# A fused attention and feed-forward kernel: list-scheduled order against an order written out, with joined small products

## The chip, the cores and the metric

The kernel runs on one core of one Trainium2 chip. The metric is the device time of one execution in microseconds (us), as the median of several runs. Before the change it is 704.83 us (three runs, 704.33 to 705.15).

## What is computed

Eight batches, each with eight heads, 576 tokens and head size 64. Per head, `phi` is turned by a softmax over the tokens into weights that compress keys and values into 32 memories; the queries attend to these memories; the heads' outputs, side by side, are the 512 features of a token, which go through a feed-forward layer 512 -> 2048 -> 512.

```python
a = softmax(phi, axis=tokens)
k_m = einsum('bhsm,bhsd->bhmd', a, k)
v_m = einsum('bhsm,bhsd->bhmd', a, v)
attn = softmax(q @ k_m.T / sqrt(64))
x = (attn @ v_m).transpose(0, 2, 1, 3).reshape(4608, 512)
h = x @ w_in
g = h * erf(softplus(h))
out = g @ w_out
```

## The kernel before

The kernel never forms `x`. For each batch it multiplies the value memories into `w_in` once ("w_in products", tile `vw` for batches 0 and 1, `wv` from batch 2 on; function `heads`, matmuls at L652), and the first layer is then that product times the attention weights (tile `at`). The unit of work is a step `i`: 16 steps per batch, each one block of 128 of the 2048 hidden features for all 576 tokens, 128 steps in all.

- **First layer.** In batches 0 and 1 `ffn1` (L850) does one step as two halves of 288 tokens; the first four steps in exact fp32, the later ones with every operand split into a high and a low part and three products. From batch 2 on `quad` (L756) does two steps together by seven products of half size instead of eight; `vw_sums` and `at_sums` make the sums that this needs.
- **Between the layers.** ScalarE does softplus (L872) and erf (L877), in groups of four steps because each of the two needs its own table loaded; VectorE multiplies by `h` (L887), and the result is split into `g` (L903 or L904, and L905).
- **Second layer.** `ffn2` (L935, tiles `pso`) adds each step's 128 features into four accumulators of 128 tokens by 512; the 64 tokens that remain of a batch go through DRAM (`rest_d`) and are done for two batches together (`ffn2_rest`, tiles `psr`).
- **Memories and attention of a batch.** `memories` and `one_memory` make the softmax of `phi` and its sums over tokens with k and v (the "sums", L598, many small matmuls), then turn them (L620) into `km` and `vm`. `attention` makes the scores (L652, from `q` and `km`) and their softmax on VectorE and ScalarE (L798 to L819), the last step of which is the transpose into `at`.
- **Weights.** They arrive as 16 chunks of 1 MB, eight of `w_in` and eight of `w_out`, in tiles `w`. A chunk lands two bytes off, so a GpSimd memset fills the last column (L426) and a DMA all the others (L428). `decode` then brings the numbers into place in three steps: a cast of every fourth 16-bit word (L485, VectorE), a scaling of the low words as integers (L486 on ScalarE or L488 on VectorE), and a merge (L480, VectorE). A decoded `w_in` chunk is also written to DRAM (L494) and read again for every later batch (L499).

Every piece of this is registered by `op(...)` as an `Op` with the engine or engines that can do it, a rank (its place in a wished order), and the tiles that it reads and writes. `Plan.order` is a list scheduler: with costs in nanoseconds it plays the program forward and at each moment gives every engine the ready piece of the lowest rank whose buffers are free. The result is one fixed order of issue per engine, and the DMA queue on SyncE (SP) is one of them. The table `SHIFT` moves the rank of single pieces. Two further rules stand in it: pieces of kind `exp` are placed only at the end of a softplus and erf group (`at_edge`), and a piece of kind `small` (sums, w_in products, scores, which use a part of the TensorE array) is preferred while TensorE is already on such pieces, since the changes to and from them are costed.

Until the first second-layer product, `fill` puts matmuls of zeros ("idle", L414) into modelled gaps of TensorE of more than 450 ns.

Of the kernel before, what the change touches and what calls it, by code (L numbers as in the profile page):

```python
# [15 lines left out]
U16 = mybir.dt.uint16  # L16
# [25 lines left out]
SHIFT = {  # L42
    "at_sums": {
        ("s", 2): 2, ("s", 3): 2,
    },
    "attention": {
        (0,): 12, (2,): 4.5, (3,): 1,
    },
    "decode": {
        ("in", 0): -9, ("in", 1): -10.5, ("in", 2): -12, ("in", 5): -11, ("in", 7): -11, ("out", 2): 11.5,  # L50
        ("out", 3): -14, ("out", 7): -0.5,
    },
    "ffn2_rest": {
        ("s", 0, 2): 5.5, ("s", 10, 2): -5.5, ("s", 12, 2): 3.5, ("s", 6, 2): 2, (7, 0, 2): -14,
    },
    "g_split": {
# [4 lines left out]
    },  # L61
    "memories": {
        (1,): 1.5, (2,): 4,
    },
    "split_wo": {
        (0,): 13, (4,): 4.5, (6,): 6,
    },
    "vw": {
        (0, 4, False): 1.5, (0, 6, False): -9.5, (1, 1, False): 0.5, (1, 5, False): 5, (1, 6, False): -5.5,
    },  # L70
    "vw_sums": {
        ("s", 3): -6.5, (2, 0): 8, (2, 1): 2.5, (2, 3): -1,
    },
}


class Op:
    def __init__(self, ways, rank, kind, nbytes, edge):
        self.ways, self.rank, self.kind, self.nbytes, self.edge = ways, rank, kind, nbytes, edge
        self.engine = next(iter(ways))  # L80
        self.before, self.after, self.tiles, self.placed = set(), [], set(), []
        self.ready = self.start = self.end = 0.0
        self.fill = 0
# [19 lines left out]

class Plan:
# [3 lines left out]
    SIGNAL = 60.0  # L108
    TABLE = 1283.0
    SWITCH = 98.0  # L110
    RELOAD = 170.0
    NEAR = 100.0

    def __init__(self, room, any_order, least, shared):
# [47 lines left out]
    def order(self):  # L162
        n_wait = {}
        for x in self.ops:
            x.rank += 100 * x.shift
            n_wait[x] = len(x.before)
            for y in x.before:
                y.after.append(x)
# [1000 lines left out]
```

## Time and profile before

| what | value |
|---|---|
| median of three runs | 704.83 us |
| the profiled execution | 704.14 us |
| its span, first to last instruction | 702.3 us |
| busy TensorE (PE) | 691.8 us (99%) |
| busy VectorE (DVE) | 581.8 us (83%) |
| busy ScalarE (ACT) | 541.9 us (77%) |
| busy GpSimd (POOL) | 30.6 us (4%) |
| moved by DMA | 115.07 MB |

The rows of the profile come from the profiled execution, whose span is 1.84 us below its own time. PE stands for matmuls and PEld for the weight loads that run beside them. Matmuls of zeros count as busy PE. SPq is the DMA queue's issuing engine. In a row with a bracket, the bracket says how long the engine was idle before and what ended that.

### The profile page before, as it was taken

How to read it: one execution, taken by the hardware profiler on the slowest of the kernel's cores; microseconds unless marked ns; L12 is line 12 of the kernel's file. 1: busy time of each engine (PE TensorE's matmuls, PEld its weight loads, DVE VectorE, ACT ScalarE, POOL GpSimd, SP SyncE). 2: the span in 40 equal slices, each digit the busy share in tenths (PEclk: the TensorE clock that was granted, in tenths of full speed). 3: DMA queues.
4: the chain of work that ended last, by engine and by line, in shares of the span. 5: the costliest groups of instructions: out<-in, count | busy, mean ns of one | idle time of the engine just before them, and what ended most of it. 6: DMA issues, size and time to landing. Idle time of an engine off the chain costs nothing.

```text
span 702.3 us, 13828 instructions
## 1 busy us (share of the span) xinstructions
PE 691.8 (99%) x5204; PEld 549.8 (78%) x5204; DVE 581.8 (83%) x1202; ACT 541.9 (77%) x978; POOL 30.6 (4%) x70
## 2 busy tenths in 40 slices
PE   8999999999999999999999999999999999999997
PEld 3566678778878888888878888788888888888885
DVE  3999999988878889998987997789998898767750
ACT  4689987977777887888878996589987895686831
POOL 0111210000000000000000000000000000011220
PEclk9999999999999999999999999999999999999999
DMA  8999953861736336273634346445321434330002
GB/s 324 415 393 421 378 186 105 289 238 34 256 106 214 102 123 227 76 236 91 250 119 139 99 147 229 128 133 191 117 76 66 122 100 139 98 110 1 1 1 75
DMA packets 71283, 115.07 MB, mean 164 GB/s; under 512 B 38064, under 2 KB 46256, under 8 KB 71216
## 3 DMA queue, kind: packets, MB, share of 16 engines
q1 hardware_dynamic: 71216, 114.18, 47.3%
q8 instruction: 41, 0.67, 0.4%
q14 instruction: 26, 0.21, 0.1%
HBM read 93.19 MB, written 20.97 MB: 163 GB/s over the span
## 4 chain that ended last, share of the span: by engine, by line
PE 90%; DMA 3%; DVE 3%; ACT 2%; SPq 1%; issue 1%; ACTq 0%; DVEq 0%
PE pso L935 48%; PE psh L756 19%; PE psh L850 7%; PE psr L935 6%; PE psa L652 6%; PE psa L598 2%; DMA q<-qT 2%; DMA phiT<-phiT 2%; PE idle L414 1%; DVE sv L677 1%; PE psa L620 0%; ACT wv L403 0%; SPq L442 0%; DVE wv L405 0%; DVE e L887 0%
## 5 line engine op out<-in xcount | busy, mean ns | idle before, releaser
L935 PE MATMUL pso<-wo,g 128*128 128x512 f32 x1440 | 392.6, 395 | 0.0
L935 PEld LDWEIGHTS pso<-wo,g 128*128 128x128 f32 x1440 | 250.4, 188 | 41.7 <-issue 7.3
L756 PEld LDWEIGHTS psh<-at,wv 128*128 128x128 f32 x1008 | 168.6, 188 | 36.5 <-DVE h L677 1.8
L756 PE MATMUL psh<-at,wv 128*128 128x288 f32 x1008 | 190.9, 298 | 1.2 <-ACT g L904 0.4
L872 ACT ACTIVATE e<-h 128x576 f32<-128x576 f32 x128 | 87.0, 685 | 38.8 <-DVE h L677 31.0
L887 DVE TENSOR_TENSOR e<-e,h 128x576 f32<-128x576 f32 x120 | 88.9, 749 | 19.7 <-ACT e L877 19.4
L905 DVE TENSOR_TENSOR g<-e,g 128x576 fp32r<-128x576 f32 x120 | 89.7, 750 | 0.6
L877 ACT ACTIVATE e<-e 128x576 f32<-128x576 f32 x128 | 84.1, 676 | 0.4
L677 DVE TENSOR_TENSOR uv<-uv,psh 128x288 f32<-128x288 f32 x96 | 43.1, 449 | 19.0 <-PE psh L756 15.8
L677 DVE TENSOR_TENSOR h<-uv,psh 128x288 f32<-128x288 f32 x96 | 43.1, 449 | 13.6 <-PE psh L756 13.0
L904 ACT ACTIVATE g<-e 128x576 fp32r<-128x576 f32 x68 | 46.5, 684 | 8.6 <-PE pso L935 4.1
L935 PE MATMUL psr<-wo,rr 128*128 128x512 f32 x192 | 49.5, 393 | 0.0
L850 PE MATMUL psh<-at_hi,vw 128*128 128x288 f32 x224 | 45.1, 306 | 0.8 <-DVE sc L798 0.8
L771 ACT ACTIVATE uv<-psh 128x288 f32<-128x288 f32 x96 | 38.9, 405 | 8.8 <-PE psh L756 8.0
L872 ACT ACT_TABLE_LOAD x33 | 42.3, 1283 | 3.9 <-DVE h L677 3.4
L877 ACT ACT_TABLE_LOAD x33 | 42.3, 1283 | 0.6
L935 PEld LDWEIGHTS psr<-wo,rr 128*128 128x128 f32 x192 | 34.8, 188 | 6.8 <-issue 0.4
L850 PEld LDWEIGHTS psh<-at_hi,vw 128*128 128x128 f32 x224 | 35.0, 188 | 5.9 <-issue 2.1
L914 POOL CAST rr<-g 128x64 fp32r<-128x64 f32 x32 | 14.0, 447 | 579.9 <-DVE g L903 550.6
L652 PE MATMUL psa<-wi,vm 64*32 64x256 f32 x1024 | 37.1, 383 | 0.0
L984 ACT ACTIVATE ot<-pso 128x512 f32<-128x512 f32 x32 | 18.5, 604 | 20.0 <-PE pso L935 19.7
L403 ACT ACTIVATE wv<-sv 128x512 fp32r<-128x512 f32 x48 | 27.8, 624 | 5.6 <-DVE sv L677 5.3
(88 smaller groups left out, 809.8 us busy)
## 6 DMA issues: line engine op xcount, KB each, us to landing
wi<-w_in_d SPq DMA_DIRECT2D x56, 512.0 KB, 4.6
kv<-kv SPq DMA_DIRECT2D x32, 640.0 KB, 9.1
q<-qT SPq DMA_DIRECT2D x16, 576.0 KB, 6.9
out<-ot SPq DMA_DIRECT2D x32, 256.0 KB, 3.5
w<-w_in SPq DMA_DIRECT2D x8, 1023.8 KB, 14.4
w<-w_out SPq DMA_DIRECT2D x8, 1023.8 KB, 13.6
rr<-rest_d SPq DMA_DIRECT2D x28, 256.0 KB, 3.4
rest_d<-g SPq DMA_DIRECT2D x104, 64.0 KB, 1.7
```

The costliest lines, as they stand in the source:

```text
L403: lambda: nc.scalar.activation(get_hi(), get_src(), AF.Identity))
L652: nc.tensor.matmul(out=get(ps[par])[p * M : (p + 1) * M, m * n : (m + 1) * n], lhsT=w[rows, p, :], rhs=get(x)[rows, p, :], start=True, sto ...
L677: op(DVE, on_dve(n) + extra, rank, reads, [o], lambda: nc.vector.tensor_tensor(out=get_o(), in0=get_x(), in1=get_y(), op=kind))
L756: nc.tensor.matmul(out=get(ps[o]), lhsT=lhsT, rhs=rhs, start=(n < 4 and m == 0), stop=(m == 2), skip_group_check=n >= 4)
L771: lambda x=x: nc.scalar.activation(get(uv)[:, x], get(ps[x]), AF.Identity))
L850: nc.tensor.matmul(out=get(ps), lhsT=x[:, g, k % 2 * P : (k % 2 + 1) * P], rhs=y[:, g, :], start=(n + g == 0), stop=(n == len(parts) - 1 a ...
L872: last[:] = [op(ACT, on_act(S), rank, [("h", i)], [e], lambda: nc.scalar.activation(get(e), get(("h", i)), AF.Softplus), kind="softplus", ...
L877: last[:] = [op(ACT, on_act(S), rank, [e], [e], lambda: nc.scalar.activation(get(e), get(e), AF.Erf), kind="erf", edge=edge, after=last)]
L887: op(DVE, on_dve(S), rank, [e, h], [to if i >= FR2 else (t, 0)], lambda: nc.vector.tensor_tensor(out=get(t)[:, 0].bitcast(F32) if i < FR2 ...
L904: other={ACT: (on_act(S), lambda: nc.scalar.activation(get(t)[:, 0], get(e), AF.Identity))})
L905: op(DVE, on_dve(S), rank, [e, (t, 0)], [(t, 1)], lambda: nc.vector.tensor_tensor(out=get(t)[:, 1], in0=get(e), in1=get(t)[:, 0].bitcast(F ...
L935: nc.tensor.matmul(out=o, lhsT=y, rhs=z, start=(start and n == 0), stop=(stop and n == len(parts) - 1))
```

## The change

The list scheduler goes, and so do the `SHIFT` table, the buffer counts that it kept and the two rules on `exp` and on small pieces. In their place stands the order itself, as a text of 58 lines. Each number in it, coded in base 32, names the next piece: all but the lowest bit is its place among the pieces that are left, sorted by rank, and the lowest bit says whether its first or its second engine does it. The text holds 3495 numbers; the lowest bit is set in 111. The cost model stays in the program for one purpose, to compute the number of fillings.

Beside that, five edits of the pieces:

1. A weight's load is registered as reading the `end` part of the tile, so that it stands behind the memset of its last column.
2. The cast of `decode` may go to ScalarE as an ACTIVATE with Identity (a second way, costed at 2250 ns by the model).
3. Joined pieces: for batches 2 to 6 the first w_in products of batch b join the sums of batch b+1 and are issued right behind them, as one piece; for batch 1 the w_in products of every odd chunk join those of the even chunk before.
4. Fillings are possible until the last step of batch 0 instead of the first second-layer product. Once the second layer has begun they add zeros into the accumulator `pso0`, without start and stop marks.
5. Some constants of the cost model (`mm`, one ACT cost) change; these reach the program only through the count of fillings.

```diff
+WRITTEN = (
+    "AlcIAlaAAiOIAjMEEClGAlWAiOiAieEEEGEIUEESIKJILJEEEGEEGEWQWiSUiShKQQhGShEEQhAQGOEEWKhJUKhFKQEEchDGMYAAUiWXGGGi"
...
-    def op(self, engine, cost, rank, reads, writes, emit, kind=None, nbytes=0, edge=None, after=(),
-           holds=(), other=()):
-        x = Op({engine: (cost, emit), **dict(other)}, rank, kind, nbytes, edge)
-        x.shift = self.shift
+    def op(self, engine, cost, rank, reads, writes, emit, kind=None, nbytes=0, after=(), other=(), join=None):
+        x = join or Op({engine: (cost, emit), **dict(other)}, rank, kind, nbytes)
+        if join:
+            (was, first), x.rank = x.ways[engine], max(x.rank, rank)
+            x.ways[engine] = (was + cost, lambda: (first(), emit()))
         x.before.update(after)
...
+        left, out = sorted(self.ops, key=lambda x: x.rank), []
+        free, landed = dict.fromkeys(ENGINES, 0.0), 2200.0
+        clock, filling, small, table = Clock(), True, False, None
+        for n in numbers(WRITTEN):
+            x = left.pop(n >> 1)
+            e = list(x.ways)[n & 1]
+            cost, x.emit = x.ways[e]
+            now = max([free[e]] + [y.end for y in x.before])
...
+        o = get(("pso", 0, 0)) if idle[1:] else idle[0] if idle else None
         for _ in range(n):
             nc.tensor.matmul(
-                out=idle[0].rearrange("p (n c) -> p n c", c=P), lhsT=zeros,
-                rhs=zeros.unsqueeze(1).to_broadcast([P, DM // P, P]), start=True, stop=True,
+                out=o.rearrange("p (n c) -> p n c", c=P), lhsT=zeros,
+                rhs=zeros.unsqueeze(1).to_broadcast([P, DM // P, P]),
+                start=not idle[1:], stop=not idle[1:], skip_group_check=len(idle) > 1,
             )
...
         load(rank, P * 8190, [(key, "top"), (key, "low")],
-             lambda: nc.sync.dma_start(out=get(key)[:, : 8 * DM - 1], in_=src[:, c].bitcast(U16)[:, 1:]))
+             lambda: nc.sync.dma_start(out=get(key)[:, : 8 * DM - 1], in_=src[:, c].bitcast(U16)[:, 1:]), [(key, "end")])
...
         op(DVE, 1330, rank, [(key, "top")], [(key, "top")],
-           top(lambda y, x: nc.vector.tensor_copy(out=y, in_=x)))
+           top(lambda y, x: nc.vector.tensor_copy(out=y, in_=x)),
+           other={ACT: (2250, top(lambda y, x: nc.scalar.activation(y, x, AF.Identity)))})
...
+    def partner(what, b, c=0):
+        if what == "vw" and c == 0 and JOIN <= b < B - 1:
+            return small["sums", b + 1]
+        return small["vw", b, c - 1] if what == "vw" and b == 1 and c % 2 else None
...
-           kind="stop filling" if k == 0 else None)
+           kind="stop filling" if i == NK - 1 else None)
```

## Rows read from the trace of the kernel before

**Rows 1.** The page: busy engines, then TensorE's granted clock in 40 slices.
```profile
PE 691.8 (99%) x5204; PEld 549.8 (78%) x5204; DVE 581.8 (83%) x1202; ACT 541.9 (77%) x978; POOL 30.6 (4%) x70
...
PEclk9999999999999999999999999999999999999999
```

**Rows 2.** PE's groups: count | busy us, mean ns | idle before, releaser.
```profile
L756 PE MATMUL psh<-at,wv 128*128 128x288 f32 x1008 | 190.9, 298 | 1.2 <-ACT g L904 0.4 <-ACT bias L521 0.3 <-DVE wv L405 0.3
L850 PE MATMUL psh<-at_hi,vw 128*128 128x288 f32 x224 | 45.1, 306 | 0.8 <-DVE sc L798 0.8
L935 PE MATMUL pso<-w,g 128*128 128x512 f32 x64 | 29.8, 600 | 1.0 <-PE psh L850 1.0
L414 PE MATMUL idle<-zeros 128*128 128x512 bf16 x76 | 20.5, 420 | 1.0 <-DVE zeros L395 1.0
```

**Rows 3.** Stretches of 20 us: busy us (instructions), PE clock, DMA share, GB/s.
```profile
0.00:20.00 20.00, 17.38 (x241) 8.40 (x241) 8.24 (x19) 8.54 (x16) 0.81 (x9) 1.00 0.91 336
20.00:40.00 20.00, 20.00 (x138) 11.77 (x131) 19.30 (x29) 14.64 (x24) 3.29 (x9) 1.00 1.03 401
40.00:60.00 20.00, 19.03 (x103) 10.93 (x103) 19.52 (x28) 17.78 (x27) 3.01 (x6) 1.00 1.01 412
60.00:80.00 20.00, 20.00 (x189) 13.39 (x188) 19.26 (x31) 18.86 (x30) 7.42 (x10) 1.00 1.02 390
80.00:100.00 20.00, 20.00 (x146) 13.25 (x145) 18.90 (x29) 16.85 (x30) 2.05 (x4) 1.00 0.87 295
```

**Rows 4.** PE in order of time, 20 to 44 us: start us, us, work, count.
```profile
21.75 4.06 PE L414 MATMUL idle<-zeros 128*128 128x512 bf16 x18
...
26.34 4.06 PE L414 MATMUL idle<-zeros 128*128 128x512 bf16 x18
...
31.15 7.92 PE L850 MATMUL psh<-at,vw 128*128 128x288 f32 x32
```

**Rows 5.** DVE in order of time, 14 to 32 us.
```profile
21.76 0.75 DVE L812 TENSOR_TENSOR sc<-sc,srs 128x576 f32<-128x576 f32 x1
22.43 1.31 DVE L485 CAST w<-w 128x1024 f16<-128x1024 bf16 x1
...
26.11 2.47 DVE L485 CAST w<-w 128x1024 f16<-128x1024 bf16 x2
...
30.03 0.72 DVE L819 STREAM_TRANSPOSE at<-sc 128x576 f32<-128x576 f32 x1
```

**Rows 6.** DVE's and ACT's groups of the decode and nearest to it.
```profile
L485 DVE CAST w<-w 128x1024 f16<-128x1024 bf16 x16 | 21.1, 1330 | 0.0
...
L486 ACT ACTIVATE w<-w 128x1024 int32<-128x1024 uint32 x13 | 18.4, 1435 | 1.6 <-DMA w<-w_in 1.6
...
L403 ACT ACTIVATE wo<-w 128x1024 fp32r<-128x1024 f32 x8 | 8.4, 1054 | 0.4 <-DVE wo L405 0.4
```

**Rows 7.** ACT in order of time, 14 to 32 us.
```profile
14.31 1.80 ACT L486 ACTIVATE w<-w 128x1024 int32<-128x1024 uint32 x1 [1.55 <-DMA w<-w_in]
```

**Rows 8.** PE in order of time: small pieces at 85, 174 and 502 us.
```profile
84.70 0.66 PE L652 MATMUL psa<-wi,vm 64*32 64x256 f32 x16
85.29 0.53 PE L850 MATMUL psh<-at_hi,vw 128*128 128x288 f32 x2
...
174.41 2.40 PE L598 MATMUL psa<-kv,phi 116*32 116x128 f32 x80
176.74 1.09 PE L652 MATMUL psa<-wi,vm 64*32 64x256 f32 x32
...
501.71 1.09 PE L652 MATMUL psa<-wi,vm 64*32 64x256 f32 x32
502.73 2.40 PE L598 MATMUL psa<-kv,phi 116*32 116x128 f32 x80
```

**Rows 9.** POOL in order of time, 26 to 32 us.
```profile
26.79 1.83 POOL L426 MEMSET w<- 128x1 uint16 x1 [25.37 <-DMA w<-w_in]
```

**Rows 10.** Waits of the DMA queue: who waited for whom, us in total, times, longest.
```profile
SPq L428 <- POOL w L426: 12.5, 3, 6.4
```

More of the change, by code (lines that the diff above doesn't have):

```diff
@@ L37, with __init__ @@
 }
[L42 to L56, printed above, removed]
[4 rows of a table removed]
[L61 to L74, printed above, removed]
-class Op:
[L78 to L83, printed above, removed]
+class Op:
+    def __init__(self, ways, rank, kind, nbytes):
+        self.ways, self.rank, self.kind, self.nbytes = ways, rank, kind, nbytes
+        self.before, self.end, self.fill = set(), 0.0, 0
 class Clock:
@@ L101, in to @@
         self.at = t
[L104 to L130 removed]
+DIGITS = "ABCDEFGHIJKLMNOPQRSTUVWXYZabcdefghijklmnopqrstuvwxyz0123456789+-"
@@ L153, in op @@
         x.before.discard(x)
-        for k in x.tiles:
-            if k in self.users:
-                self.users[k].append(x)
-                x.placed.append(k)
-        x.placed += [k for k in holds if k not in x.tiles]
-        self.ops.append(x)
+        if not join:
+            self.ops.append(x)
         return x
     def order(self):
[L163 to L168, printed above, removed]
@@ L169, in order @@
-        room, turn = dict(self.room), dict.fromkeys(self.turn, 0)
-        left = {k: len(u) for k, u in self.users.items()}
-        waiting = {e: [x for x in self.ops if e in x.ways and not n_wait[x]] for e in ENGINES}
-        free = dict.fromkeys(ENGINES, 0.0)
-        table, at_edge, small = None, True, False
-        landed, clock, filling = 2200.0, Clock(), True
-        releases, out, now, held = [], [], 0.0, set()
-        def fits(x):
-            need = {}
-            for k in x.placed:
-                if k in held:
-                    continue
-                p = self.pool_of[k]
-                if p not in self.any_order and self.turn[p][turn[p] + need.get(p, 0)] != k:
-                    return False
-                need[p] = need.get(p, 0) + 1
-            if any(room[p] < n for p, n in need.items()):
-                return False
-            return not any(p in self.least for p in need) or self.shared >= sum(
-                max(n, self.room[p] - room[p] + need.get(p, 0)) for p, n in self.least.items())
@@ L250, in order @@
                 late = 60.0
-            x.cost = cost
             free[e] = now + cost
-            x.start, x.end = now, now + cost + late
+            x.end = now + cost + late + self.SIGNAL
             if e == SP:
@@ L256, in order @@
                 landed = begin + x.nbytes / (250 if x.nbytes < 1.2e5 else 340 if begin < 13000 else 385)
-                x.end = landed + 900
+                x.end = landed + 900 + self.SIGNAL
             out.append(x)
-            for y in x.after:
-                n_wait[y] -= 1
-                y.ready = max(y.ready, x.end + self.SIGNAL)
-                if not n_wait[y]:
-                    for w in y.ways:
-                        waiting[w].append(y)
-            for k in x.tiles:
-                if k in left:
-                    left[k] -= 1
-                    if not left[k]:
-                        end = max(u.end for u in self.users[k]) + self.SIGNAL
-                        heapq.heappush(releases, (end, len(out) * 16 + len(releases), self.pool_of[k]))
+        assert not left
         return out
@@ L760, in product @@
             chain[:] = [op(PE, 3 * mm(U, False), rank + (0 if n < 4 else 60) + 0.1 * n,
-               [(w, (m, a_part)) for m in range(2)] + [at_] + ([] if n < 4 else [ps[o]]), [ps[o]], emit,
-               holds=h + [uv] if n == 0 else (), after=chain)]
+               [(w, (m, a_part)) for m in range(2)] + [at_] + ([] if n < 4 else [ps[o]]), [ps[o]], emit, after=chain)]
         def half(r, u):
@@ L856, in emit @@
                     )
-        op(PE, (2 if exact else 6) * mm(U, exact), rank, [w] + ats, [ps], emit, holds=[h])
+        op(PE, (2 if exact else 6) * mm(U, exact), rank, [w] + ats, [ps], emit)
         def keep():
```

190 lines of the change are left out of this document (98 added, 92 removed), and 4 rows, old and new, of the table SHIFT.

## The prediction

> **What bounds the kernel now.** I read the page first. TensorE is busy 691.8 us of a span of 702.3, VectorE 581.8, ScalarE 541.9, and TensorE's granted clock shows its top tenth in all 40 slices, the 2.4 GHz level [rows 1]. So the kernel is bound by what TensorE is given to do, with 10.5 us in which it does nothing. I then asked TensorE's groups what it was idle for [rows 2]. Three groups hold idle time after the start: 1.2 us before the quads' products, 0.8 before the first layer of the early batches, 1.0 before the exact second layer. That is 3.0 us in the whole body. Two parts are outside: the end, where the last result is copied and stored, which the change leaves as it is, and the start.
>
> The start is where busy deceives. The matmuls of zeros count as busy, 20.5 us of them [rows 2]. TensorE's order of time shows two long runs of 18, at 21.75 and 26.34 us, 4.06 us each, and the first product of the first layer only at 31.15 us [rows 4]. Together the two runs are 8.1 us in which nothing else could be done. Why it could not is in VectorE's order of time: the softmax of the first 288 tokens is multiplied out at 21.76 us, but its transpose into `at`, which the first layer reads, stands at 30.03 us, behind three casts of the decode (1.31 us and 2.47 for two) and other work that is queued between [rows 5]. The stretches of 20 us say that this is no lone accident of order: from 20 to 100 us VectorE is busy 19.30, 19.52, 19.26 and 18.90 us, 77.0 of 80, and the DMA share is at or near one until 80 us [rows 3]. ScalarE has more room, 68.1 of 80 in the same four rows. So up to 100 us VectorE is the second bound beside TensorE; later it is TensorE alone.
>
> **The change part by part.**
>
> *The cast on ScalarE.* Sixteen casts take 21.1 us of VectorE, 1.33 each [rows 6]. Each one moved takes 1.33 us off the engine that holds up the start. How many move is coded in the text: its lowest bit is set in 111 of 3495 numbers, and the bit also serves other pieces that have two ways, so the count is some of the sixteen, not all. No row shows this cast on ScalarE. The nearest is the integer step of the same decode, on the same 128x1024 words with the same kind of stride: 1.435 us in the mean [rows 6], 1.80 the longest single one [rows 7]; a plain copy of 128x1024 takes 1.054 [rows 6]. I take 1.44, since the stride is what it shares with the integer step, and keep 1.05 and 1.80 as ends.
> What it buys: from 20 to 40 us ScalarE is idle 5.4 us (20 less 14.64) [rows 3], in pieces between the softmax and the products' copies. Two casts of 1.44 fit there, three if they fit without delaying an exp. Two take 2 x 1.33 = 2.7 us from the queue ahead of the transpose. I count three quarters of that, 2.0 us, because part of the work around it will wait for ScalarE instead. Is an earlier start kept? From 20 to 100 us VectorE has 3.0 us to spare without any move (80 less 77.0), so a start 2.0 us earlier can be fed. The ends: nothing, if another gate takes over, and 8.1 us, if both runs of zeros go; a loss is a rival below.
> The Trainium skill (ScalarE: Activation LUTs, What ACT_TABLE_LOAD costs) gives an ACTIVATE with immediate scale and bias 186 ns and 0.833 ns per element, 1.04 us for 1024 as an estimate. The plain copy's 1.054 us agrees and the integer step's 1.435 does not [rows 6]; by the page a third cast would fit from 20 to 40 us and the sum would be up to 1.3 us lower. The same page's Rules for kernel authors send simple operations to VectorE, as up to about three times faster in bf16 for ops with a single source, which speaks against the move; here VectorE needs 1.33 us for 1024 numbers, so the row shows no such lead.
>
> *The written order.* It can only reorder; no product of the two layers goes away. What it can win in the body is the 3.0 us of idle time [rows 2], three different waits (a split on VectorE, an attention transpose, the start of the second layer). I count a third, 1.0 us; ends: 3.0 gained, and 2.0 lost if the fixed order puts a product before its operand about as often as the old one did, plus again half.
>
> *The joined pieces.* Between batches 2 and 6 the sums and the first w_in products are to be adjacent. They already are: the first of these pairs runs from 174.41 to 176.74 us and on, the last from 501.71 over 502.73, with nothing between, and so do the three between [rows 8]. Those five joins buy nothing; in the last, the order of the two turns round, so the w_in products come 2.33 us later (176.74 less 174.41), covered by the products that stand ready in the queue at that point. New are the four pairs of batch 1. A lone piece of 16 takes 0.59 us (84.70 to 85.29), a double one 1.02 (501.71 to 502.73) [rows 8]: 2 x 0.59 - 1.02 = 0.16 us, four times 0.6 us. I take 0.6. Ends: 1.2 gained if the change back to full products is saved as well, and 1.2 lost if one pair waits for its second chunk: the pair stands in TensorE's queue, and everything behind it waits.
>
> *Loads behind memsets.* A load now never stands ahead of its memset, so GpSimd's queue is ahead of SyncE's. In the old order three loads already waited for one, 12.5 us in total, 6.4 the longest [rows 10], and one memset stood 25.4 us until a load had landed and then took 1.83 us [rows 9]. A memset can run once its buffer is free, which the load needs too. Behind a waiting load stand the later loads, and the decodes wait for these. I take nothing, since the DMA share is one anyway until 80 us [rows 3] and a load issued later still finds a full queue; ends: 0 and 1.8 us lost, one such slow memset ahead of a load that is needed.
>
> *Fillings through batch 0.* The granted clock is already at its top level in every slice [rows 1], so more zeros win nothing there. They cost where a gap is shorter on the chip than planned, at 4.06 / 18 = 0.23 us each [rows 4]. After the start TensorE's idle time in batch 0 is at most the 1.8 us of two rows [rows 2], room for 8 at the most. I take nothing; ends: 0 and 1.8 lost.
>
> **The sum.** 2.0 + 1.0 + 0.6 = 3.6 us off the profiled execution: 704.14 - 3.6 = 700.5. The median of the runs is 0.7 us above that execution, so the forecast in medians is 704.83 - 3.6 = 701.2 us.
>
> **The rivals.**
> *The start goes almost whole.* The order puts the transpose of the first half right behind its multiplication and moves the casts away, and both runs of zeros shrink to a little. For it: between 22.5 and 30.0 us nothing that the transpose reads is missing [rows 5]. Against it: VectorE has 3.0 us to spare until 100 us, so a start 6.5 us earlier needs 3.5 us off it, 2.6 casts, and each stage behind has to be early too. Price: 6.5 + 1.0 + 0.6 = 8.1 us, 696.7.
> *No change.* The start moves but the weights' arrival does not: the DMA share is 0.91, 1.03, 1.01, 1.02 up to 80 us [rows 3], so TensorE starts early and stalls at a later chunk. Then the start gives nothing, and 1.0 + 0.6 remain less some new waits: 704.0, with 703.4 to 706.2 as its own width.
> *ScalarE becomes the bound, slower.* From 40 to 100 us it is busy 17.78, 18.86 and 16.85 us, with 6.5 us to spare [rows 3]. Softplus and erf stand in its queue behind a cast, and the second layer waits for these. At 1.80 us each the room is gone with the fourth cast placed there, and the 3.6 us of the forecast are gone too from the sixth ((6.5 + 3.6) / 1.8 = 5.6). With seven casts there: 7 x 1.8 - 6.5 = 6.1 late, less 3.6: 707.3.
> *It does not do what it says.* In part that is already in the sum: five of nine joins are adjacent as they were [rows 8]. If no cast moves, only order is left, and that is the case of no change.
>
> **How the numbers follow.** The forecast, with its own range of 699 to 703.4, has 0.42; the start gone almost whole 0.18; no change 0.20; slower 0.20. A difference of 0.2%, 1.4 us, is about what a measurement of this kernel can tell. So faster 0.60, same 0.20, slower 0.20. The range reaches down to 695.0, past the first rival with part of the remaining idle time of the body, and up to 707.0, just short of the slower rival's 707.3; about one in ten is left out on each side.
>
> **What would show it.** Right: the busy time of the zeros falls below 18 us and the first product of the first layer starts before 30 us; a new row of ACT casting `w`, at 1.05 to 1.80 us; VectorE's casts fewer than 16; double w_in pieces in batch 1; less than 3.0 us of idle time in the body. Wrong: the first product early but a new wait of TensorE for `g` or a weight between 40 and 100 us (no change); ScalarE over 19.5 of 20 us there with TensorE idle (slower); a SyncE wait on memsets longer than 6.4 us with a decode behind it. What would undo the whole working is a change after 160 us, where TensorE alone is the bound and I expect little.

## The result

| | before | after |
|---|---|---|
| median of four runs each | 704.58 us (704.11 to 705.15) | 698.97 us (697.52 to 699.11) |
| profiled execution, its span | 704.14, 702.3 us | 699.04, 697.2 us |
| TensorE busy (share) | 691.8 us (99%) | 685.5 us (98%) |
| VectorE busy | 581.8 us | 585.9 us |
| ScalarE busy | 541.9 us | 540.7 us |

The ratio after to before is 0.9917, with an interval of 0.9900 to 0.9934: faster by 5.6 us, where 3.6 was forecast.

Line numbers below are those of the changed kernel: L356 a zero, L428 and L429 the cast on VectorE and ScalarE, L430 and L432 the integer step on ScalarE and VectorE, L423 the merge, L369 a memset, L371 a weight's load, L604 the small products, L542 the sums, L802 and L709 the first layer, L887 the second; in the changed kernel's variants the same lines stand a few numbers further on. First the page of after, to be held against [rows 1] (the granted clock again shows its top tenth in all slices), and its groups of TensorE, against [rows 2] (count | busy, mean ns | idle before):

```profile
PE 685.5 (98%) x5185; PEld 550.5 (79%) x5185; DVE 585.9 (84%) x1223; ACT 540.7 (78%) x962; POOL 24.3 (3%) x70
...
L802 PE MATMUL psh<-at_hi,vw 128*128 128x288 f32 x224 | 43.4, 304 | 0.0
L604 PE MATMUL psa<-wi,vm 64*32 64x256 f32 x1024 | 36.3, 383 | 1.2 <-DMA wi<-w_in_d 1.1
...
L542 PE MATMUL psa<-kv,phi 116*32 116x128 f32 (+3 forms) x720 | 19.6, 262 | 1.9 <-DVE sc L755 1.5 <-DMA kv<-kv 0.3
L356 PE MATMUL idle<-zeros 128*128 128x512 bf16 x57 | 16.2, 429 | 1.0 <-DVE zeros L336 1.0
```

The span, 5.1 us shorter, comes apart on these rows. The zeros are 57 instead of 76, 16.2 us instead of 20.5: 4.3 less. All other work of TensorE is 669.3 us (685.5 less 16.2) instead of 671.3: 2.0 less. Idle time is 11.7 us (697.2 less 685.5) instead of 10.5: 1.2 more. -4.3 - 2.0 + 1.2 = -5.1. The 2.0 us repeat: in four traces of the changed order with the joins in place or one pair apart (after, a_same, a_pair0, a_first4) the other work is 669.2 to 669.4 us. (In a_swap, a_best, a_memset and a_rest7 it is 670.2 to 672.6, in the last three with a lower granted clock in a stretch.) Two old waits have no row any more (the first layer's for `sc`, the second's start); new are 1.1 us for `wi<-w_in_d` and, in this execution alone (a_same has none), 0.9 us for `h` ahead of the small bias products at 400.74 us.

Where in the span this lies is in the stretches of after (busy of PE, PEld, DVE, ACT, POOL with their instruction counts, then PE's clock, DMA share, GB/s), against [rows 3]:

```profile
0.00:20.00 20.00, 16.87 (x242) 8.02 (x243) 9.79 (x25) 7.67 (x18) 1.15 (x15) 1.00 0.91 340
20.00:40.00 20.00, 19.35 (x143) 12.02 (x142) 18.95 (x30) 19.61 (x26) 0.41 (x4) 1.00 1.00 373
40.00:60.00 20.00, 20.00 (x116) 12.82 (x115) 19.00 (x31) 19.93 (x27) 4.17 (x8) 1.00 0.89 330
60.00:80.00 20.00, 20.00 (x178) 12.59 (x177) 19.03 (x32) 18.39 (x28) 2.67 (x8) 1.00 0.88 343
80.00:100.00 20.00, 18.61 (x136) 11.96 (x135) 18.72 (x32) 19.85 (x31) 3.20 (x4) 1.00 0.94 304
```

Until 40 us TensorE is idle 3.8 us instead of 2.6, but with 4.3 us fewer zeros: 3.1 us won (2.3 by the same sum in a_same, another execution of this kernel). From 40 to 60 us the old wait of 0.97 us is gone. From 80 to 100 us 1.4 us are lost again. That leaves 2.7 us of saved zeros and idle time at 100 us, and 0.4 more come after it. The other 2.0 us are the shorter work, which these stretches do not place. ScalarE, which I had at 68.1 of 80 us from 20 to 100, is now at 77.8, 97%; VectorE is at 75.7 instead of 77.0.

The order of time shows the start: TensorE and then VectorE of after (start, length, work, count, and in brackets the idle time before it), against [rows 4] and [rows 5]:

```profile
11.91 1.55 PE L604 MATMUL psa<-q,km 64*32 64x288 f32 x32 [0.21 <-ACT km L578]
...
20.45 3.40 PE L356 MATMUL idle<-zeros 128*128 128x512 bf16 x15
...
24.38 0.82 PE L356 MATMUL idle<-zeros 128*128 128x512 bf16 x3
25.55 1.24 PE L802 MATMUL psh<-at,vw 128*128 128x288 f32 x4 [0.36 <-ACT vw L623]
...
43.13 2.31 PE L887 MATMUL pso<-w,g 128*128 128x512 f32 x5
```

```profile
19.61 0.69 DVE L432 TENSOR_SCALAR w<-w 128x1024 int32<-128x1024 uint32 x1 [0.39 <-DMA w<-w_in]
20.23 1.42 DVE L764 TENSOR_TENSOR sc<-sc,srs 128x576 f32<-128x576 f32 x2
22.24 1.23 DVE L423 SCALAR_TENSOR_TENSOR wi<-w 128x1024 uint32<-128x1024 uint32 x1 [0.60 <-issue]
23.38 0.77 DVE L771 STREAM_TRANSPOSE at<-sc 128x576 f32<-128x576 f32 x1
```

The first product of the first layer stands at 25.55 us instead of 31.15. The scores of both halves are done together at 11.91 us, where in before those of the second half come at 19.41, after a wait of 0.42 for `q`. So the softmaxes of both halves run side by side (counts of 2) with no cast between them, and the first transpose stands at 23.38 instead of 30.03. Executions of one kernel differ here: in a_same the first product stands at 26.55, so a difference of one microsecond at the start shows nothing. The row of a_same:

```profile
26.55 1.24 PE L802 MATMUL psh<-at,vw 128*128 128x288 f32 x4 [0.35 <-ACT vw L623]
```

The second layer starts at 43.13, in after, as early as before (43.23): what was won is that first-layer products are done ahead of it instead of zeros. The last three zeros are at 24.38 us, so the longer reach of the fillings added none.

Last, the decode in after (VectorE's and ScalarE's groups), against [rows 6]:

```profile
L429 ACT ACTIVATE w<-w 128x1024 f16<-128x1024 bf16 x11 | 27.9, 2536 | 0.4 <-DMA w<-w_in 0.4
L432 DVE TENSOR_SCALAR w<-w 128x1024 int32<-128x1024 uint32 x15 | 10.9, 738 | 1.1 <-DMA w<-w_in 1.1
L428 DVE CAST w<-w 128x1024 f16<-128x1024 bf16 x5 | 6.6, 1321 | 0.0
L430 ACT ACTIVATE w<-w 128x1024 int32<-128x1024 uint32 x1 | 1.1, 1133 | 0.0
```

Eleven casts run on ScalarE, at 2.54 us each, outside the ends of 1.05 to 1.80 that I gave. And something I had not read in the change: the integer step, 13 of 16 on ScalarE before, is now 15 of 16 on VectorE, since its way is written in the text too. Decode steps cost ScalarE 29.0 us instead of 18.4.

### The profile page after: what moved, and what is told of

Same layout as the page of the kernel before. It is cut to its first block, busy times and chain, and to the rows that moved or that the text cites. A ratio compares the mean times of both kernels' runs of the same rounds, so it can differ in the third digit from the quotient of the medians.

```text
span 697.2 us, 13725 instructions
## 1 busy us (share of the span) xinstructions
PE 685.5 (98%) x5185; PEld 550.5 (79%) x5185; DVE 585.9 (84%) x1223; ACT 540.7 (78%) x962; POOL 24.3 (3%) x70
## 4 chain that ended last, share of the span: by engine, by line
PE 82%; DMA 7%; DVE 4%; ACT 3%; SPq 2%; issue 1%; DVEq 0%
PE pso L887 45%; PE psh L709 19%; PE psr L887 6%; PE psa L604 5%; PE psh L802 4%; PE psa L542 2%; DMA phi<-phi 2%; DMA w<-w_in 2%; DMA out<-ot 2%; ACT w L429 1%; DMA w_in_d<-wi 1%; DMA wi<-w_in_d 1%; DVE w L423 1%; SPq L861 1%; SPq L385 1%
## 5 line engine op out<-in xcount | busy, mean ns | idle before, releaser
L887 PE MATMUL pso<-wo,g 128*128 128x512 f32 x1440 | 386.8, 395 | 0.0
L887 PEld LDWEIGHTS pso<-wo,g 128*128 128x128 f32 x1440 | 252.6, 188 | 42.3 <-issue 5.7
L709 PEld LDWEIGHTS psh<-at,wv 128*128 128x128 f32 x1008 | 168.2, 188 | 36.5 <-DVE h L630 3.3
L709 PE MATMUL psh<-at,wv 128*128 128x288 f32 x1008 | 191.3, 298 | 0.9 <-ACT h L730 0.5
L824 ACT ACTIVATE e<-h 128x576 f32<-128x576 f32 x128 | 84.4, 682 | 19.0 <-DVE h L630 13.5
L344 ACT ACTIVATE wv<-psa 128x256 fp32r<-128x256 f32 (+1 forms) x96 | 28.5, 337 | 28.5 <-PE psa L604 23.4
L887 PE MATMUL psr<-wo,rr 128*128 128x512 f32 x192 | 49.5, 393 | 0.0
L856 ACT ACTIVATE g<-e 128x576 fp32r<-128x576 f32 x52 | 35.4, 680 | 14.2 <-DVE e L839 11.1
L802 PE MATMUL psh<-at_hi,vw 128*128 128x288 f32 x224 | 43.4, 304 | 0.0
L887 PEld LDWEIGHTS psr<-wo,rr 128*128 128x128 f32 x192 | 34.8, 188 | 7.0 <-issue 0.4
L604 PE MATMUL psa<-wi,vm 64*32 64x256 f32 x1024 | 36.3, 383 | 1.2 <-DMA wi<-w_in_d 1.1
L802 PEld LDWEIGHTS psh<-at_hi,vw 128*128 128x128 f32 x224 | 34.3, 188 | 3.3 <-issue 2.3
L346 DVE TENSOR_TENSOR wv<-psa,wv 128x128 fp32r<-128x128 f32 (+1 forms) x96 | 32.1, 347 | 2.9 <-ACT wv L344 2.8
L855 DVE CAST g<-e 128x576 fp32r<-128x576 f32 x68 | 30.8, 453 | 3.5 <-DMA rest_d<-g 1.4
```

Source lines behind the costliest of these rows:

```text
L346: lambda: nc.vector.tensor_tensor(out=get_lo(), in0=get_src(), in1=get_hi().bitcast(F32), op=ALU.subtract))
L604: nc.tensor.matmul(out=get(ps[par])[p * M : (p + 1) * M, m * n : (m + 1) * n], lhsT=w[rows, p, :], rhs=get(x)[rows, p, :], start=True, sto ...
L709: nc.tensor.matmul(out=get(ps[o]), lhsT=lhsT, rhs=rhs, start=(n < 4 and m == 0), stop=(m == 2), skip_group_check=n >= 4)
L802: nc.tensor.matmul(out=get(ps), lhsT=x[:, g, k % 2 * P : (k % 2 + 1) * P], rhs=y[:, g, :], start=(n + g == 0), stop=(n == len(parts) - 1 a ...
L824: last[:] = [op(ACT, on_act(S), rank, [("h", i)], [e], lambda: nc.scalar.activation(get(e), get(("h", i)), AF.Softplus), kind="softplus", ...
L856: other={ACT: (on_act(S), lambda: nc.scalar.activation(get(t)[:, 0], get(e), AF.Identity))})
```

## The experiments

Three questions: did the casts win the start, what are the joins worth, and is the order of memsets and loads free? Ratios are to the kernel before on the same chip; the changed kernel's own are 0.9917 (0.9900 to 0.9934) and, run again beside the last kernels, 0.9908 (a_same below). Unless a text says so, a kernel computes all of the result.

### Is it the casts?

**a_swap**: the changed kernel, the eleven casts back on VectorE and their integer steps back on ScalarE, at the same places of the order.

```diff
+    for cast, whole in pairs:
+        if cast.emit is cast.ways[ACT][1]:
+            cast.emit = cast.ways[DVE][1]
+            whole.emit = whole.ways[ACT][1]
```

> The changed kernel with its written order, but in the eleven chunks whose cast stands on ScalarE the cast goes to VectorE and the integer step to ScalarE, as the kernel before had it in 13 of 16 chunks. Theory 1 (the engine: taking the casts off VectorE is what brings the start forward): VectorE gets 11 x (1.33 - 0.72) = 6.7 us more to do before 100 us, the first product starts two us or more later than 25.55 us, and the time rises by 3 to 4 us against the changed kernel, to 702 to 703. Theory 2 (the order: the softmax of the first batch runs on VectorE without decode steps between, and q is loaded ahead of the weights; where the casts run matters little, since a cast on ScalarE takes 2.52 us there): the first product stays within one us of 25.55 and the time within 1 us of the changed kernel's 699.0, or below it, since ScalarE gets 11 x (2.52 - 1.44) = 11.9 us less to do.

Measured: 700.54 us, ratio 0.9936 (0.9912 to 0.9961). Without any cast on ScalarE, 4.5 us of gain are left; by the medians' ratios the split of the decode is worth some 1.3 us (2.0 against a_same), an amount that the intervals don't settle. The first product comes at 26.84 us, 1.3 later than in after but only 0.3 later than in a_same, where the last load of `kv` came as late. More is lost further on: VectorE is full (19.96 of 20 us from 80 to 100), and at 102.03 us TensorE has waited 2.24 us for the next weight, where after waits 1.13. A stretch of a_swap, then TensorE at that place:

```profile
80.00:100.00 20.00, 19.79 (x202) 13.62 (x200) 19.96 (x35) 14.75 (x25) 7.71 (x8) 1.00 0.77 252
```

```profile
102.03 0.67 PE L605 MATMUL psa<-wi,vm 64*32 64x256 f32 x16 [2.24 <-DMA wi<-w_in_d]
```

**a_first4 and a_rest7** halve that: the same edit for the first four of the eleven (19 to 32 us), and for the other seven (42 to 95 us).

```diff
+    moved.sort(key=lambda t: order.index(t[0]))
+    for cast, whole in moved[:4]:    # a_rest7: moved[4:]
+        cast.emit = cast.ways[DVE][1]
+        whole.emit = whole.ways[ACT][1]
```

> The changed kernel with the cast back on VectorE and the integer step on ScalarE in the first four of the eleven chunks alone (those that run between 19 and 32 us). If what counts is the start, where these steps lie between the softmax and the first products: most of what all eleven cost, 1.5 to 2 us slower than 699.0. If what counts is VectorE's work summed up to 100 us: the four's share, 4/11 of the 1.6 us (medians) to 2.9 us (traces) that all eleven cost, 0.6 to 1.1 us.

> The same for the other seven chunks alone (from 32 us on). If what counts is the start: within 0.5 us of 699.0, or faster, since ScalarE, busy 19.85 of 20 us from 80 to 100, gets less to do. If what counts is VectorE's sum: 7/11, 1.0 to 1.9 us slower.

Measured: a_first4 698.28 us, ratio 0.9919 (0.9891 to 0.9948); a_rest7 700.14 us, 0.9936 (0.9910 to 0.9961), where a_swap was. By the intervals neither is told apart from after. My step was that two casts fewer between 20 and 40 us bring the transpose forward. With all four back there, the first product stands at 25.84 us. One trace settles little here, so I take all: in the seven with the four early casts on ScalarE it stands at 24.58 to 26.59 us, the middle one at 25.53; in the three with them on VectorE at 25.84, 26.84 and 27.60; in the old order at 31.15 in before and 31.95 in b_cast. So the order won most of the start, 3.5 us or more, and the four casts may be worth about one, which is not seen in a_first4's time. That the later casts count is likely but not shown: a_rest7 has VectorE full and waits 1.81 us for the next weight, against 1.13 in after and 1.42 in a_same. a_rest7 from 40 to 60 us, then TensorE at 98 us:

```profile
40.00:60.00 20.00, 19.85 (x110) 11.91 (x109) 19.96 (x31) 15.69 (x26) 6.24 (x8) 1.00 0.76 278
```

```profile
98.69 0.67 PE L605 MATMUL psa<-wi,vm 64*32 64x256 f32 x16 [1.81 <-DMA wi<-w_in_d]
```

**b_start**: an early start alone, in the kernel before: both loads of `q` first, and the shift that holds back batch 0's attention taken out.

```diff
-        (0,): 12, (2,): 4.5, (3,): 1,
+        (2,): 4.5, (3,): 1,
...
-    FIRST = ["phiT0", "phiT1", "k0", "k1", "q0", "in0", "v0", "v1", "q1", "in1", "out0"]
+    FIRST = ["phiT0", "phiT1", "k0", "k1", "q0", "q1", "v0", "v1", "in0", "in1", "out0"]
```

> The kernel before, with two of its own settings moved toward the written order's start and nothing else: both q loads ahead of the value and weight loads, and no shift of the first attention's rank. Theory 2 (the order): its first product starts before 28 us, not at 31.15, and it is 2 to 4 us faster, 701 to 703. Theory 1 (VectorE has no room): the first product starts earlier, but TensorE waits as much between 30 and 100 us and the time stays within 1 us of 704.6.

Measured: 712.73 us, ratio 1.0123 (1.0093 to 1.0153): slower by 8. TensorE in order of time (the lines are those of the kernel before), and one stretch:

```profile
25.43 4.15 PE L850 MATMUL psh<-at,vw 128*128 128x288 f32 x16
...
30.69 2.33 PE L414 MATMUL idle<-zeros 128*128 128x512 bf16 x10
...
40.20 3.84 PE L414 MATMUL idle<-zeros 128*128 128x512 bf16 x17
...
44.25 1.03 PE L935 MATMUL pso<-w,g 128*128 128x512 f32 x2
...
88.00 1.34 PE L652 MATMUL psa<-q,km 64*32 64x288 f32 x9 [2.25 <-ACT km L634]
```

```profile
80.00:100.00 20.00, 15.36 (x172) 10.31 (x171) 19.68 (x29) 17.59 (x32) 2.61 (x4) 0.83 0.76 277
```

The first product is as early as in after, 25.43 us, and it is worth nothing here. There are zeros again at 30.69, as the second half's softmax stands behind casts on VectorE (its multiplication comes at 31.15), and at 40.20, as the second layer's operand `g` is not multiplied out before 43.24; the second layer starts at 44.25. From 80 to 100 us TensorE has 4.6 us without work. So an early first product is not enough; the later stages have to be fed earlier too, and in the written order more of the first layer is done when the second starts.

**b_cast**: the kernel before with the cast's second way and nothing else.

```diff
-           top(lambda y, x: nc.vector.tensor_copy(out=y, in_=x)))
+           top(lambda y, x: nc.vector.tensor_copy(out=y, in_=x)),
+           other={ACT: (2250, top(lambda y, x: nc.scalar.activation(y, x, AF.Identity)))})
```

> The kernel before with one part of the change alone: the cast may go to ScalarE, at the cost of 2250 ns that the change gives it, and the list scheduler decides. If the engine is what brings the gain: 1.6 to 2.9 us faster than 704.6, 702 to 703. If the gain needs the order written with it (the old ranks and shifts were set for the old durations): no gain, 704 to 708.

Measured: 704.22 us, ratio 0.9996 (0.9982 to 1.0009). The list scheduler put all sixteen casts on VectorE, so this run says that the edit alone does nothing there, and nothing about casts on ScalarE under that scheduler.

**a_price**: what the cast costs on ScalarE, by itself: behind the last result of the changed kernel seven forms of ACTIVATE, each twice, on spare buffers of 128x1024 numbers. It does more than the reference asks, so its total of 718.58 us is no time to compare.

```diff
+            nc.scalar.activation(b16.bitcast(F16), a16.bitcast(BF16), AF.Identity)
+            nc.scalar.activation(vb[:, :1024].bitcast(F16), va[:, :1024].bitcast(BF16), AF.Identity)
+            nc.scalar.activation(vb[:, :1024].bitcast(F16), a16.bitcast(BF16), AF.Identity)
+            nc.scalar.activation(b16.bitcast(F16), va[:, :1024].bitcast(BF16), AF.Identity)
+            nc.scalar.activation(vc, a16.bitcast(BF16), AF.Identity)
+            nc.scalar.activation(b16.bitcast(F16), vc, AF.Identity)
+            nc.scalar.activation(b32.bitcast(I32), a32, AF.Identity, scale=LOW)
```

> The changed kernel with 14 ScalarE instructions behind its last result, on memory that nothing else uses any more: seven forms of a pass over 128x1024, twice each. It measures the cast's cost by itself (2.52 us in the changed kernel against 1.44 for the integer step, with the same stride of 8 bytes). If it is the stride of the 16-bit source: a cast from the strided source to a packed target takes 2.5 us too. If it is the stride of the 16-bit target: a cast from a packed source to the strided target takes 2.5 us. If it is the type: a packed cast takes 2.5 us. Otherwise each takes about 1.05 us, as a plain copy of 128x1024 does. The time itself is some 25 us longer and says nothing.

ScalarE's groups of a_price. The seven forms have lines 1071 to 1077 in the order of the diff; `a16`, `b16`, `a32` and `b32` take one number of every 8 bytes:

```profile
L1076 ACT ACTIVATE vb<-vc 128x1024 f16<-128x1024 f32 x2 | 4.9, 2474 | 0.1
L1074 ACT ACTIVATE vb<-va 128x1024 f16<-128x1024 bf16 x2 | 4.9, 2470 | 0.1
L1071 ACT ACTIVATE vb<-va 128x1024 f16<-128x1024 bf16 x2 | 4.9, 2450 | 0.0
...
L1077 ACT ACTIVATE vb<-va 128x1024 int32<-128x1024 uint32 x2 | 2.3, 1149 | 0.0
...
L1073 ACT ACTIVATE vb<-va 128x1024 f16<-128x1024 bf16 x2 | 2.2, 1107 | 0.1
L1072 ACT ACTIVATE vb<-va 128x1024 f16<-128x1024 bf16 x2 | 2.1, 1056 | 0.1
```

The three forms that write 16-bit numbers 8 bytes apart take 2.45 to 2.47 us, wherever the source lies and whatever its type. Reading with that stride costs little (1.107 against 1.056 us), and writing 32-bit numbers with it is 1.149. So it is the 16-bit target with a stride, not the stride as such. The page of before has the integer step at 1.435 in the mean for another reason, as far as its trace goes: nine steps that ran beside a cast on VectorE for more than 0.9 us took 1.38 to 1.80, the other four 1.15 to 1.21. Two of them, the first beside the cast at 22.43 in [rows 5], the second beside none:

```profile
22.44 1.77 ACT L486 ACTIVATE w<-w 128x1024 int32<-128x1024 uint32 x1
...
88.21 1.17 ACT L486 ACTIVATE w<-w 128x1024 int32<-128x1024 uint32 x1
```

No run tried the two apart, and a_swap and a_rest7 have one step each that took 1.17 beside a cast all along.

### What are the joins worth?

**a_unjoin and a_pair0**: the changed kernel; the second part of a joined piece is held back on TensorE. In a_unjoin that is each of the nine, by one piece; in a_pair0 only the first pair of batch 1, the one that waits at 97 us in after, by two.

```diff
+        if held and (x.keys & held.second or (PE in x.ways and left == 0)):
+            held.parts[1]()
+            held = None
+        if x.parts and count == 0:      # a_unjoin: every x.parts, left = 1
+            x.parts[0]()
+            held, left = x, 2
```

> The changed kernel, but in all nine joined pieces the second part is issued one TensorE piece later (three to six full products stand between). If being adjacent is worth the 0.16 to 0.3 us per pair that the prediction counts: 9 x 0.25 = 2.2 us slower, less the 1.1 us that the pair at 95 us no longer waits for its second chunk, so about +1.1 us, 700.1. If being adjacent is worth nothing (the changes to and from small pieces are hidden): 1.1 us faster, 697.9.

> The changed kernel, but in the one pair of batch 1 where TensorE was idle 1.13 us for the second chunk's load (97.09 us in its trace) the second part is issued two TensorE pieces later. If the joined piece's wait is a net loss: 1.13 less about 0.25 for the change to small pieces, 0.9 us faster, 698.1. If the wait is taken from slack (another wait appears behind it): within 0.3 us of 699.0.

Measured: a_unjoin 702.28 us, ratio 0.9956 (0.9941 to 0.9971), 3.3 slower than after by the medians (4.2 than a_same); a_pair0 696.78 us, 0.9880 (0.9864 to 0.9897), 2.2 faster than after (1.3 than a_same, with whose interval its own just overlaps). TensorE of after at the pair, then of a_pair0, then the page of a_unjoin:

```profile
95.30 0.66 PE L604 MATMUL psa<-wi,vm 64*32 64x256 f32 x16
97.09 0.67 PE L604 MATMUL psa<-wi,vm 64*32 64x256 f32 x16 [1.13 <-DMA wi<-w_in_d]
```

```profile
95.21 0.66 PE L607 MATMUL psa<-wi,vm 64*32 64x256 f32 x16
95.80 1.65 PE L890 MATMUL pso<-wo,g 128*128 128x512 f32 x6
97.38 0.66 PE L607 MATMUL psa<-wi,vm 64*32 64x256 f32 x16
```

```profile
PE 687.4 (98%) x5185; PEld 549.3 (78%) x5185; DVE 585.9 (84%) x1223; ACT 541.1 (77%) x962; POOL 24.4 (3%) x70
```

Six products that were ready go between the two parts, and the second chunk has landed by then. The wait of 1.13 us accounts for about half of the 2.2; the spans differ by 1.8 (697.2 and 695.4). In a_unjoin one piece between is not enough there (0.63 us of wait are left), and another pair's shift brings a wait of 1.00 us for `vw` ahead of the sums at 118.93 us. What a change to small pieces and back costs can be read from the page: less 15.1 us of zeros, TensorE's other work is 672.3 us, 3.0 more than in after over nine pairs, 0.33 each and twice the 0.16 that I counted. By that price the four pairs of batch 1 would be 1.3 of the 2.0 us of work that the change saved; this is an estimate, and a_pair0, with one of them apart, has only 0.1 us more work (669.4).

**b_join**: the same joins in the kernel before, under its list scheduler.

```diff
+        x = join or Op({engine: (cost, emit), **dict(other)}, rank, kind, nbytes, edge)
+        if join:
+            (was, first), x.rank = x.ways[engine], max(x.rank, rank)
+            x.ways[engine] = (was + cost, lambda: (first(), emit()))
...
+        small[key] = op(PE, 4 * n * len(xs) / 2.4, rank, [(memory, b % 2)] + xs, ps, emit, kind="small",
+                        holds=holds, join=partner(*key))
```

> The kernel before with the joined pieces alone, ordered by its list scheduler. By the prediction's count 0.6 us faster, 704.0 (four pairs of batch 1 by 0.16 us; the five others were adjacent already). Rival: a joined piece has to wait for the later of its operands and holds up TensorE behind it, as at 97 us in the changed kernel: 1 us or more slower, 705.6 and up.

Measured: 736.07 us, ratio 1.0446 (1.0413 to 1.0479), 31 us slower. Until 100 us it runs as before; from 140 us on TensorE waits again and again, 10.3 us ahead of the quads alone. As I read it, a joined piece takes its rank from the later of its two parts, and what waits for the earlier one comes late; that was not tried apart. TensorE of b_join at the first long wait, and a stretch further on:

```profile
146.51 0.53 PE L863 MATMUL psh<-at_hi,vw 128*128 128x288 f32 x2 [3.05 <-DVE vw L410]
```

```profile
260.00:280.00 20.00, 15.22 (x102) 12.30 (x104) 10.91 (x21) 12.27 (x17) 0.00 (x0) 0.83 0.12 26
```

### Is the order of memsets and loads free?

**a_memset**: the changed kernel with every memset right behind its load instead of ahead of it.

```diff
-        op(POOL, 100, rank, [], [(key, "end")], lambda: nc.gpsimd.memset(get(key)[:, 8 * DM - 1 :], 0))
+        op(POOL, 100, rank, [], [(key, "end")], lambda: None)
...
-             lambda: nc.sync.dma_start(out=get(key)[:, : 8 * DM - 1], in_=src[:, c].bitcast(U16)[:, 1:]), [(key, "end")])
+             lambda: (nc.sync.dma_start(out=get(key)[:, : 8 * DM - 1], in_=src[:, c].bitcast(U16)[:, 1:]),
+                      nc.gpsimd.memset(get(key)[:, 8 * DM - 1 :], 0)), [(key, "end")])
```

> The changed kernel with every weight's memset issued right behind its load instead of ahead of it, nothing else. If the order of the two is hidden, as the prediction counts it: within 0.5 us of the changed kernel. If the load's or the decode's wait for the memset counts: the memset then waits for the landing, GpSimd's queue stands until then, and the decode's merge comes later, 1 us or more slower.

Measured: 701.72 us, ratio 0.9951 (0.9929 to 0.9973), 3.7 slower than a_same on the same chip. Waits of a_memset (us in total, times, longest), then GpSimd, the DMA queue, ScalarE and TensorE in order of time:

```profile
POOL w L372 <- DMA w<-w_in: 39.6, 8, 18.0
```

```profile
78.47 0.10 POOL L372 MEMSET w<- 128x1 uint16 x1 [7.88 <-ACT h L818]
78.59 0.41 POOL L850 CAST rx<-g 128x64 fp32r<-128x64 f32 x2
...
79.31 0.87 SPq L862 DMA_DIRECT2D rest_d<-rx  x2
...
80.78 0.93 SPq L391 DMA_DIRECT2D q<-qT  x2
...
91.08 0.69 ACT L857 ACTIVATE g<-e 128x576 fp32r<-128x576 f32 x1 [3.05 <-POOL rx L851]
...
85.48 0.72 PE L605 MATMUL psa<-q,km 64*32 64x288 f32 x16 [2.24 <-ACT vm L579]
...
100.27 0.67 PE L605 MATMUL psa<-wi,vm 64*32 64x256 f32 x16 [2.33 <-DMA wi<-w_in_d]
```

A memset behind its load waits until the load has landed, and GpSimd's other work stands behind the memset: the casts of `rx` that carry the last 64 tokens. (At 78.47 us the profile names ScalarE's `h` as the releaser; the chunk, issued at 71.60, landed 6.8 us later, 0.1 us ahead of the memset, which speaks for the load.) `rx` is late, so is its store in the DMA queue, and with the store what is queued behind it: in after the loads of `q` stand at 78.38 us and the scores start at 83.71 after a wait of 0.26, here at 80.78 and 85.48. (The profile names `vm` as the releaser; that the first part of `q` landed 4.6 us after its issue, 0.1 us before the scores start, speaks for the load.) ScalarE, too, waits for `rx` to be read out of `g`, and the chunk for the second of the pair at 97 us comes later as well, after a wait of 2.33 us instead of 1.13. Until 80 us TensorE runs as in after; from 80 to 100 it is busy 15.70 us instead of 18.61. This is the extreme, with all sixteen turned round; in the kernel before, the two orders were mixed.

### The changed kernel once more, and both finds together

**a_same** is the changed kernel again, run five times; **a_best** is a_pair0 and a_first4 in one.

> The changed kernel itself once more, beside the others of this call on the same chip, since runs of one program differ here by up to 3 us. Expected: 699.0 within 1 us, 0.8% below the kernel before.

> The changed kernel with two edits that the earlier runs point to: the pair at 95 us taken apart (second part two TensorE pieces later), and the first four casts back on VectorE with their integer steps on ScalarE. If the two gains stand beside each other: 2.2 us and 0.7 us, 696.1. If the first four casts make no difference: 696.8.

Measured: a_same 698.05 us, ratio 0.9908 (0.9891 to 0.9924); a_best 697.82 us, 0.9904 (0.9884 to 0.9924), six runs from 696.78 to 700.93. The two finds don't add up. Its profiled execution is the longest of the six: the pair's wait is gone there, but the first-layer products start at 27.60 us, two us later than in after and one later than in a_same, TensorE having waited 0.87 and 0.55 us for VectorE's `wi` at 25.79 and 29.36 us. Its granted clock until 20 us was 0.91, too, where after had 1.00. TensorE of a_best at its start:

```profile
25.79 0.86 PE L608 MATMUL psa<-wi,vm 64*32 64x256 f32 x16 [0.87 <-DVE wi L426]
...
27.60 1.21 PE L806 MATMUL psh<-at,vw 128*128 128x288 f32 x4 [0.20 <-DVE at L775]
```

Whether the four casts back on VectorE cost something at the start, and whether a_best falls short of a_pair0 in general, its spread leaves open.

## Why the prediction was right, and where its steps failed

The sign and the size were right: 698.97 us within the forecast's own range of 699 to 703.4 but for 0.03 us, and within the full one. The mechanism was half right, and that the sum came within 2.0 us of the 5.6 is in part luck: the start's gain had another cause than the one I summed, the body's came in work and not in waits, and a loss at the pair stood against both.

**The start (-2.0 forecast).** In place and direction right: the zeros fell from 20.5 to 16.2 us, the first product moved from 31.15 to 25.55, net 3.1 us until 40 us (2.3 in a_same). The cause was not the one I gave. "Each one moved takes 1.33 us off the engine that holds up the start" failed as the main cause: with the four early casts back on VectorE the first product still stands 3.5 to 5.3 us ahead of before (27.60 to 25.84 against 31.15), and the time is not told apart (a_first4). The order did it, `q` loaded first and the softmaxes of both halves ahead of most of the decode on VectorE; b_start gets the same early first product from the order of before with the `q` loads and one rank moved. That was my first rival's mechanism ("puts the transpose of the first half right behind its multiplication and moves the casts away"). Against it I had put VectorE's 3.0 us to spare until 100 us; b_start shows that an early start can be lost again, as it was in that order. Whether the later casts on ScalarE help to keep the lead is not settled: 1.2 us (a_rest7) to 1.6 us (a_swap) by the medians, inside the intervals.

**The price of the cast.** I took 1.44 with ends of 1.05 and 1.80, "since the stride is what it shares with the integer step". It measured 2.54. The integer step by itself is 1.149 in a_price, so its 1.435 in [rows 6] was not the stride's price either; the longer ones ran beside VectorE's casts. The estimate from the Trainium skill (ScalarE: Activation LUTs, What ACT_TABLE_LOAD costs), 186 ns and 0.833 ns per element whatever the type, 1.04 us for 1024, agrees with the packed cast's 1.056 and not with the strided 16-bit target's 2.45. The rule of the Trainium skill that simple operations belong on VectorE (ScalarE: Activation LUTs, Rules for kernel authors; it lists `relu`, `add` and the like and no cast), which I set aside since "the row shows no such lead", agrees with this cast's rows: 1.32 us on VectorE, 2.54 on ScalarE. Whether the move pays all the same, VectorE being the fuller engine, is the 1.3 us that a_swap doesn't settle.

**ScalarE becomes the bound (rival).** Its condition, six casts at 1.80 from 40 to 100 us, was passed: after the first four, seven casts at 2.54 stand between 42 and 95 us. Its price did not come. I had counted ScalarE's load as it was and not looked at what else the lowest bit could do: twelve of thirteen integer steps left it in exchange, which I take for the reason. ScalarE is busy 77.8 of 80 us from 20 to 100 us, and no group of matmuls names it for a wait of more than 0.5 us. I had said that ScalarE above 19.5 of 20 from 40 to 100 us "with TensorE idle" would show "slower"; it stood at 19.93 and 19.85 in two of the three stretches, in the second with TensorE idle 1.4 us, most of it for a weight and not for ScalarE, and the kernel was faster.

**No change (rival).** Its mechanism came in small: the wait of 1.13 us for the chunk at 97 us takes back part of the 4.1 us won until 60 us.

**The written order in the body (-1.0).** Idle time from 40 us on, the end included, is 7.9 us before and after (10.5 less 2.6, 11.7 less 3.8). Gone are the waits of 0.97 and 0.84 us; new are 1.13 for the pair's chunk and 0.9 for `h` at 400 us. What came instead is 2.0 us less of other work on TensorE. The groups don't tell in which products: the second layer's (`pso<-wo,g`) fall most, from 392.6 to 386.8 us at the same count and mean, the first layer's `at_hi` by 1.7 and the w_in products by 0.8, but groups overlap at their ends, so one that is broken less often shows less. By a_unjoin's price the joins of batch 1 make some 1.3 of it; the rest stays open. The gain that I looked for in waits lay in shorter work.

**The joins (-0.6, ends -1.2 and 1.2).** Half right. The five later joins were adjacent already, though the order of the two parts was turned round in four of them and not in the last alone (w_in products at 257.21 us, sums at 258.23, for one). The price per pair was undersized, 0.16 us against 0.33 in a_unjoin. The loss that I named as an end, "if one pair waits for its second chunk", happened, at 1.13 us, and taking that pair apart makes the kernel 2.2 us faster than after, 1.3 than a_same (a_pair0). The other pairs are worth having: with all nine apart it is 3.3 us slower (a_unjoin).

**Loads behind memsets (0, ends 0 and 1.8 lost).** The size was wrong for a reason that I had the row for. In [rows 9] a memset stood 25.4 us until a load had landed; I asked only who waits for the memset, and not what is queued behind it on GpSimd. The opposite order costs 3.7 us (a_memset), so the edit protects from more than I allowed. The sign that I gave did not come in after: there the DMA queue waits for a memset once, 1.0 us. How much of it the change won against the mixed order of before was not measured.

**Fillings (0).** Right: none was added.

## What to carry to other kernels

An early start is worth what the following stages can be fed: compare the place at which the next layer starts and what is done before it, not the first product alone. Before a microsecond at one place of a trace is called an effect, look at the same place in a second execution of the same kernel. When a change gives an operation a second engine, list every operation that can now change engines, and price a strided write from a row with the same target width; a row with the same stride only is not near enough. And for a tiny operation on a side queue, ask what stands behind it there, not only who waits for its result.

## What the runs showed of the hardware

ScalarE writes 16-bit numbers 8 bytes apart at 2.45 to 2.47 us for 128x1024, 2.3 times the 1.06 us of a packed target; a 32-bit target with the same stride takes 1.15. VectorE needs 1.32 us for the strided 16-bit cast.

On before's integer steps the company of a cast on VectorE goes with 1.38 to 1.80 us instead of 1.15 to 1.21; why is open.

TensorE's granted clock fell in stretches in which it was starved: 0.83 in b_start's with 15.36 us of work in 20, and 0.83 in b_join's with 15.22, where 1.00 is the 2.4 GHz level. In a_memset it was 0.91 from 100 to 120 us, with TensorE at work for 19.73 of these 20 us, right behind the stretch with 15.70: so part of the products after a long wait ran slower too. At after's waits, 1.4 us in 20, the clock stayed at 1.00.
